# The last output tile of a fused attention and feed-forward kernel: three column pieces, each stored from two queues

## The chip, the cores and the metric

One core of one Trainium2 chip. The metric is the device time of one execution in microseconds (us); the profile's span of the same execution is 1.7 to 1.8 us shorter. Every set of timed runs of a version was taken on the same chip as runs of the kernel before, in turns.

## The reference

A linear attention with cosine weights, whose output is the input of a feed-forward block:

```python
# q, k, v: (8, 8, 576, 64)
q_p, k_p = phi(q), phi(k)                      # relu, times cos and sin of the position: 128 features
kv  = einsum('bhsf,bhsd->bhfd', k_p, v)
x   = einsum('bhsf,bhfd->bhsd', q_p, kv) / (einsum('bhsf,bhf->bhs', q_p, k_p.sum(2)) + 1e-6)
x   = x.transpose(0, 2, 1, 3).reshape(4608, 512)
h   = x @ w_in                                 # 512 -> 2048
out = (h / (1 + exp(-beta * h))) @ w_out       # 2048 -> 512, fp32, (4608, 512)
```

## The kernel before

The 4608 tokens pass in nine chunks of 512. For each chunk TensorE makes 16 groups of `h` (four matmuls of 512 columns each), ScalarE turns each into a bf16 activation tile `g_t`, and TensorE then makes four output tiles of 128 tokens (16 matmuls of 512 columns each). An output tile holds two groups of 64 tokens that lie in different rows of the result, so it is stored in two halves of 64 rows. TensorE leaves its results in a memory called PSUM (`ps` in the code); VectorE or ScalarE copies them from there to a tile `o_sb` in SBUF, the core's working memory, from which the stores take them. The very last tile of the last chunk is made in two column pieces of 256, so that the first piece can be copied out and stored while the second is computed:

```python
    def store(c, tt, o_sb, m0=0, m1=512):
        for hf in range(2):
            bb, n = divmod((c * TCH + tt * P) // HP + hf, NQ)
            eng = nc.sync if c >= 7 else nc.gpsimd
            eng.dma_start(out=out_v[bb, n][:, m0:m1], in_=o_sb[hf * HP : (hf + 1) * HP, m0:m1])
    # ... cut ...
    def o_last(c, tt):
        o_sb = osb_pool.tile([P, DM], FP32, name="o_sb", tag="o_sb")
        for hf in range(2):
            m0, m1 = 256 * hf, 256 * hf + 256
            o_ps = ps[:, 4 + hf, 0:256]
            for jt in range(JT):                                   # 16
                nc.tensor.matmul(o_ps, lhsT=gs[c, jt][:, tt * P : (tt + 1) * P],
                                 rhs=wout[jt // 4][:, jt % 4, m0:m1],
                                 start=(jt == 0), stop=(jt == JT - 1))
            (nc.scalar.copy if hf == 0 else nc.vector.tensor_copy)(o_sb[:, m0:m1], o_ps)
            store(c, tt, o_sb, m0, m1)
```

Of the kernel before, what the change touches and what calls it, by code (L numbers as in the profile page):

```python
# [22 lines left out]
def kernel(  # L23
# [14 lines left out]
    nc = tc.nc  # L38
# [26 lines left out]
    ps = psum.tile([P, 8, 512], FP32, name="ps")  # L65
# [313 lines left out]

    out_v = out.rearrange("(b p n) m -> b n p m", b=B, n=NQ)  # L380

    def store(c, tt, o_sb, m0=0, m1=512):
        for hf in range(2):
            bb, n = divmod((c * TCH + tt * P) // HP + hf, NQ)
            eng = nc.sync if c >= 7 else nc.gpsimd
            eng.dma_start(out=out_v[bb, n][:, m0:m1], in_=o_sb[hf * HP : (hf + 1) * HP, m0:m1])  # L386

    def o_part(c, tt, part):
        o_ps = ps[:, (2, 3, 0, 1)[tt] if c == 0 else 2 + tt % 2]
        for jt in range(4 * part, 4 * part + 4):  # L390
            nc.tensor.matmul(o_ps, lhsT=gs[c, jt][:, tt * P : (tt + 1) * P],  # L391
                             rhs=wout[jt // 4][:, jt % 4, :],
                             start=(jt == 0), stop=(jt == JT - 1))
        if part < 3:
            return
        o_sb = osb_pool.tile([P, DM], FP32, name="o_sb", tag="o_sb")
        nc.scalar.copy(o_sb, o_ps)  # L397
        store(c, tt, o_sb)

    def o_last(c, tt):  # L400

        o_sb = osb_pool.tile([P, DM], FP32, name="o_sb", tag="o_sb")
        for hf in range(2):
            m0, m1 = 256 * hf, 256 * hf + 256
            o_ps = ps[:, 4 + hf, 0:256]
            for jt in range(JT):
                nc.tensor.matmul(o_ps, lhsT=gs[c, jt][:, tt * P : (tt + 1) * P],  # L407
                                 rhs=wout[jt // 4][:, jt % 4, m0:m1],
                                 start=(jt == 0), stop=(jt == JT - 1))
            (nc.scalar.copy if hf == 0 else nc.vector.tensor_copy)(o_sb[:, m0:m1], o_ps)  # L410
            store(c, tt, o_sb, m0, m1)


    def warm_pe(count, w=512, bank=1):
# [170 lines left out]
    for c in range(1, NTC):  # L585
        units = att_units(c + 1) if c + 1 < B else []
        for slot in range(32):
            if c == 1 and slot < 4:
                h_mm(c, slot, (2, 3))
                h_act(c, slot)  # L590
            elif slot < 16:
                h_group(c, slot)
            elif c == NTC - 1 and slot >= 28:
                if slot == 28:
                    o_last(c, 3)
            else:
                o_part(c, (slot - 16) // 4, slot % 4)
            while units and units[0][0] <= slot:
                units.pop(0)[1]()
# [30 lines left out]
```

## Time and profile before

| | before |
|---|---|
| time, median of 3 runs | 296.96 us (296.57 to 296.97) |
| span of the profiled run | 294.99 us |
| TensorE busy | 97% of the span |
| last tile, first weight load to last matmul's end | 3.87 us |
| from there to the end of the span (the tail) | 4.21 us |

The prediction below shows the lines that carry this. In them, a chain line reads: start, length, what. A timeline line reads: start, length, engine, source line, operation, and in brackets how long the engine had been idle and who released it. "SPq" is SyncE's queue, "ACTq" ScalarE's; a DMA line's length is that of the issue, not of the transfer, whose end is given as "DMA to landing". "DVEq" is likewise VectorE's queue, here an instruction that only waits. A row of one source line reads: line, engine, operation, count, then shortest, median and longest duration in ns and the first and last start. A row of a stretch reads: from, to and length, the busy time of each engine with its number of instructions, the granted clock, and in the last two columns the DMA engines' share and GB/s. Where this document gives times to the nanosecond, they are read from the start, end and landing records of the same traces.

### The profile page before, as it was taken

How to read it: one execution, taken by the hardware profiler on the slowest of the kernel's cores; microseconds unless marked ns; L12 is line 12 of the kernel's file. 1: busy time of each engine (PE TensorE's matmuls, PEld its weight loads, DVE VectorE, ACT ScalarE, POOL GpSimd, SP SyncE). 2: the span in 40 equal slices, each digit the busy share in tenths (PEclk: the TensorE clock that was granted, in tenths of full speed). 3: DMA queues.
4: the chain of work that ended last, by engine and by line, in shares of the span. 5: the costliest groups of instructions: out<-in, count | busy, mean ns of one | idle time of the engine just before them, and what ended most of it. 6: DMA issues, size and time to landing. Idle time of an engine off the chain costs nothing.

```text
span 295.0 us, 7173 instructions
## 1 busy us (share of the span) xinstructions
PE 286.8 (97%) x3058; PEld 142.8 (48%) x3058; DVE 116.3 (39%) x296; ACT 140.1 (47%) x223; POOL 73.8 (25%) x88
## 2 busy tenths in 40 slices
PE   8799999999999999999999999999999999999994
PEld 7454455455445544454445544554455444444443
DVE  5989978662920293019500960077005000000000
ACT  5758826563247214731474137512760277137510
POOL 1350003252382026402550256015701210000000
PEclk9999999999999999999999999999999999999999
DMA  7999999597999089916992599139102810130033
GB/s 259 366 393 379 387 389 393 197 288 268 163 259 361 4 125 219 383 62 120 217 379 76 113 231 397 45 67 196 44 2 46 146 37 0 41 84 19 0 73 71
DMA packets 50256, 53.82 MB, mean 182 GB/s; under 512 B 30880, under 2 KB 31152, under 8 KB 50224
## 3 DMA queue, kind: packets, MB, share of 16 engines
q1 hardware_dynamic: 47504, 46.01, 51.6%
q0 software_dynamic: 2688, 7.34, 10.7%
q8 instruction: 24, 0.39, 0.6%
q14 instruction: 8, 0.07, 0.1%
q10 hardware_dynamic: 32, 0.01, 0.0%
HBM read 36.71 MB, written 9.44 MB: 156 GB/s over the span
## 4 chain that ended last, share of the span: by engine, by line
PE 85%; DVE 5%; DMA 5%; ACT 2%; issue 1%; DVEq 0%
PE ps L366 38%; PE ps L391 38%; DMA w_stage<-in_moe_w_out_dram 5%; DVE win L108 4%; PE ps L281 4%; PE ps L260 3%; PE ps L407 1%; PE ps L416 1%; ACT vb L213 1%; DVE qs L218 1%; DVE xs L303 0%; ACT g_t L373 0%; ACT rk L188 0%; PE ps L425 0%; PE ps L230 0%
## 5 line engine op out<-in xcount | busy, mean ns | idle before, releaser
L366 PE MATMUL ps<-xt,win 128*128 128x512 bf16 x576 | 128.1, 379 | 0.8 <-ACT g_t L373 0.5
L391 PE MATMUL ps<-wout,g_t 128*128 128x512 bf16 x560 | 124.5, 379 | 0.2 <-ACT wout L115 0.2
L373 ACT ACTIVATE g_t<-ps,beta 128x512 bf16<-128x512 f32 x144 | 98.4, 687 | 36.6 <-PE ps L366 36.6
L366 PEld LDWEIGHTS <-win 128*128 128x128 bf16 x576 | 55.3, 98 | 67.6 <-DVE win L108 1.4
L391 PEld LDWEIGHTS <-g_t 128*128 128x128 bf16 x560 | 53.9, 98 | 64.0 <-issue 0.4
L386 POOL DMA_DIRECT2D out_dram<-o_sb x56 | 36.5, 656 | 142.2 <-ACT o_sb L397 142.2
L397 ACT COPY o_sb<-ps 128x512 f32<-128x512 f32 x35 | 20.5, 586 | 98.2 <-PE ps L391 98.2
L218 POOL TENSOR_TENSOR qs<-qt,tanr 128x1152 bf16<-128x1152 bf16 x12 | 29.3, 2456 | 10.2 <-DMA qt<-qb 10.2
L272 DVE CAST kv<-ps 128x520 bf16<-128x520 f32 x6 | 4.2, 700 | 67.8 <-PE ps L260 67.8
L410 DVE COPY o_sb<-ps 128x256 f32<-128x256 f32 x1 | 0.4, 425 | 63.0 <-PE ps L407 63.0
L303 DVE TENSOR_TENSOR xs<-ps,rden 128x768 bf16<-128x768 f32 (+5 forms) x26 | 23.1, 890 | 0.8
L292 DVE TENSOR_TENSOR den<-ps,eps 128x12 f32<-128x12 f32 (+4 forms) x26 | 4.2, 161 | 33.5 <-PE ps L281 33.5
L215 DVE TENSOR_SCALAR vb<-raw_v,cos 128x256 bf16<-128x256 f32 x63 | 17.1, 347 | 0.0
L215 DVE TENSOR_SCALAR vb<-raw_v,sin 128x256 bf16<-128x256 f32 x54 | 14.7, 349 | 0.0
L281 PEld LDWEIGHTS <-qt 64*64 64x64 bf16 x576 | 10.6, 106 | 5.0 <-issue 4.3
L281 PE MATMUL ps<-kv,qt 64*64 64x65 bf16 x576 | 11.8, 195 | 0.4 <-ACT kv L270 0.2
L190 DVE TENSOR_SCALAR qb<-raw_q 128x1152 bf16<-128x1152 f32 x16 | 11.4, 752 | 1.3 <-DMA raw_q<-in_q_dram 1.3
L108 DVE CAST win<-w_stage 64x512 bf16<-64x512 f32 (+1 forms) x28 | 11.6, 414 | 0.6
L260 PE MATMUL ps<-vb,rk 64*64 64x130 bf16 x576 | 10.1, 218 | 1.6 <-ACT rk L188 1.6
L281 PE MATMUL ps<-kv,qs 64*64 64x65 bf16 x576 | 11.6, 193 | 0.0
L260 PEld LDWEIGHTS <-rk 64*64 64x64 bf16 x576 | 8.5, 106 | 5.7 <-issue 3.0
L281 PEld LDWEIGHTS <-qs 64*64 64x64 bf16 x576 | 10.4, 105 | 0.0
(56 smaller groups left out, 99.9 us busy)
## 6 DMA issues: line engine op xcount, KB each, us to landing
raw_v<-in_v_dram SPq DMA_DIRECT2D x7, 1152.0 KB, 10.2
raw_k<-in_k_dram SPq DMA_DIRECT2D x7, 1152.0 KB, 12.9
raw_q<-in_q_dram SPq DMA_DIRECT2D x7, 1152.0 KB, 7.4
out_dram<-o_sb POOLq DMA_DIRECT2D x56, 128.0 KB, 4.1
w_stage<-in_moe_w_out_dram SPq DMA_DIRECT2D x4, 1024.0 KB, 9.0
w_stage<-in_moe_w_in_dram SPq DMA_DIRECT2D x3, 1024.0 KB, 12.8
out_dram<-o_sb SPq DMA_DIRECT2D x14, 128.0 KB, 2.3
raw_q<-in_q_dram SPq DMA_DIRECT2D x2, 576.0 KB, 4.4
```

The costliest lines, as they stand in the source:

```text
L108: nc.vector.tensor_copy(o, a)
L190: nc.vector.tensor_scalar(dst, src, scalar1=0.0, scalar2=None, op0=ALU.max)
L215: nc.vector.tensor_scalar(o, a, scalar1=t[:, n : n + 1], scalar2=None, op0=ALU.mult)
L218: eng.tensor_tensor(dst.rearrange("q n (g p) -> q n g p", g=2), src.rearrange("q n (g p) -> q n g p", g=2), tanr[:, n0:n1].unsqueeze(2).to ...
L260: nc.tensor.matmul(t[jj * HP : (jj + 1) * HP, g], lhsT=rk[hs, n, 2 * jp + jj, :], rhs=vb[hs, n, 2 * jp + jj].rearrange("q s e -> q (s e)") ...
L281: nc.tensor.matmul(ps[cols, bank + jj, slot * E : (slot + 1) * E], lhsT=(qt, qs)[cs][rows, jp, n, cols], rhs=kv[rows, g, jp, cs, :], start ...
L303: nc.vector.tensor_tensor(o.rearrange("q j n s d -> q j (n s) d"), nv[:, :, a:z, :, 0:D].rearrange("q j n s d -> q j (n s) d"), rden[:, :, ...
L366: nc.tensor.matmul(ps[:, h_bank(c, jt)], lhsT=win[jt // 4][:, mi, (jt % 4) * P : (jt % 4 + 1) * P], rhs=xt[:, :, jp, g * HP : (g + 1) * HP ...
L373: nc.scalar.activation(g_t, ps[:, h_bank(c, jt)], AF.Silu, scale=beta[:, jt : jt + 1])
L386: eng.dma_start(out=out_v[bb, n][:, m0:m1], in_=o_sb[hf * HP : (hf + 1) * HP, m0:m1])
L391: nc.tensor.matmul(o_ps, lhsT=gs[c, jt][:, tt * P : (tt + 1) * P], rhs=wout[jt // 4][:, jt % 4, :], start=(jt == 0), stop=(jt == JT - 1))
L397: nc.scalar.copy(o_sb, o_ps)
```

## The change

Intent: with smaller last pieces, less is left to copy and to store when the last matmul is done; with one half on SyncE's queue and one on ScalarE's, the second half needs not wait for the first one's issue.

```diff
-    def store(c, tt, o_sb, m0=0, m1=512):
+    def store(c, tt, o_sb, m0=0, m1=512, two=False):
         for hf in range(2):
             bb, n = divmod((c * TCH + tt * P) // HP + hf, NQ)
-            eng = nc.sync if c >= 7 else nc.gpsimd
+            eng = (nc.sync, nc.scalar)[hf] if two else nc.sync if c >= 7 else nc.gpsimd
             eng.dma_start(out=out_v[bb, n][:, m0:m1], in_=o_sb[hf * HP : (hf + 1) * HP, m0:m1])
@@ o_last @@
-        for hf in range(2):
-            m0, m1 = 256 * hf, 256 * hf + 256
-            o_ps = ps[:, 4 + hf, 0:256]
+        for i, (m0, m1) in enumerate(((0, 256), (256, 384), (384, 512))):
+            o_ps = ps[:, 4 + i, 0 : m1 - m0]
             for jt in range(JT):
                 ...
-            (nc.scalar.copy if hf == 0 else nc.vector.tensor_copy)(o_sb[:, m0:m1], o_ps)
-            store(c, tt, o_sb, m0, m1)
+            (nc.scalar.copy if i == 1 else nc.vector.tensor_copy)(o_sb[:, m0:m1], o_ps)
+            store(c, tt, o_sb, m0, m1, two=True)
```

## The prediction

> **What bounds the kernel now.** I read the page's busy shares first, then the chain that ended last, then its last pieces in order of time, then the tail's rows one by one.
>
> The busy shares and the chain say what the body is bound by:
>
> ```profile
> span 295.0 us, 7173 instructions
> PE 286.8 (97%) x3058; PEld 142.8 (48%) x3058; DVE 116.3 (39%) x296; ACT 140.1 (47%) x223; POOL 73.8 (25%) x88
> ...
> PE 85%; DVE 5%; DMA 5%; ACT 2%; issue 1%; DVEq 0%
> ```
>
> TensorE is busy for 97% of the span and carries 85% of the chain. The change touches none of that body: only the last 128-row output tile (L407 to L411) and its stores. So all of the effect lies in the last 8 us. The chain in order of time gives their compute part:
>
> ```profile
> 276.93 10.36 PE ps L391 x48
> 287.29 3.51 PE ps L407 x32
> 290.80 0.03 DVEq L410
> 290.83 0.04 issue
> 290.88 0.42 DVE o_sb L410
> ```
>
> The last tile is 32 matmuls of 256 columns, 3.51 us or 109.7 ns each; then VectorE copies the second half out of PSUM, ending at 291.30. Here the chain of compute stops and the stores take over. The last two issues on SyncE's queue (a timeline of that queue for 291.3 to 291.6, then one of all engines for 291.5 to 292 and for 291.85 on), and the stores' own rows by stretch:
>
> ```profile
> 291.33 0.47 SPq L386 DMA_DIRECT2D out_dram<-o_sb  x1
> ...
> 291.85 0.59 SPq L386 DMA_DIRECT2D out_dram<-o_sb  x1
> ```
>
> ```profile
> L386 SPq DMA_DIRECT2D out_dram<-o_sb x1: 588/588/588, 291.8 to 291.8; - x1
> DMA to landing us min/median/max: 2.0/2.0/2.0
> ```
>
> The two 64-row halves are issued one after the other, 0.52 us apart; the second lands 2.0 us after its start, at 293.85. Five stretches of the tail show the rest:
>
> ```profile
> 292.44:293.00 0.56, 0.00 (x0) 0.00 (x0) 0.00 (x0) 0.00 (x0) 0.00 (x0) 1.00 0.49 117
> 293.00:293.40 0.40, 0.00 (x0) 0.00 (x0) 0.00 (x0) 0.00 (x0) 0.00 (x0) 1.00 0.62 148
> 293.40:293.85 0.45, 0.00 (x0) 0.00 (x0) 0.00 (x0) 0.00 (x0) 0.00 (x0) 1.00 0.06 14
> 293.85:295.00 1.15, 0.00 (x0) 0.00 (x0) 0.00 (x0) 0.00 (x0) 0.00 (x0) 1.00 0.00 0
> ```
>
> The last two columns are the DMA engines' share and GB/s: the bytes move between 292.44 and 293.4, so the issue itself and the confirmation, not the bandwidth, fill the 2.0 us. From 293.85 to 295.0 only closing waits, drains and semaphores run. The tail therefore adds up: 290.80 (last matmul) + 0.08 (hand-over) + 0.42 (copy) + 0.03 (hand-over) + 0.52 (first issue) + 2.0 (second store) + 1.15 (closing) = 295.0.
>
> **What the Trainium skill says.**
> - "DMA: Bandwidth & Descriptors", section "Issuing engines are not separate DMA queues": stores issued from several engines run on the same 16 DMA engines, and only the sequencer's issue time is saved. Here that time is the 0.52 us between the two issues; the trace of before never stores from two of these queues in the tail, so it can't confirm it.
> - "Perfetto Trace Analysis", section "DMA Instruction — HWDGE (DVE, Sync)": the block that generates descriptors is shared by the issuing sequencers and locked for exclusive use, and the profiled window includes the wait for the lock. If so, two stores issued at once partly queue. The trace hints at something like it: in each pair the second issue takes 587 to 589 ns against 466 of the first.
> - "TensorE: Matmul & The Clock Gate", section "Back-to-back issue gap": columns/2.4 + 2.5 ns apart when isolated (109 ns at 256 columns, which agrees with 109.7; 56 ns at 128), but some 81 ns per matmul in a real stream of weight load and matmul at 128 columns. The trace's own 128-column bursts decide below.
> - "VectorE: DVE Perf Modes", section on the TRN2 errata: a PSUM to SBUF copy costs a fixed term plus the columns. The trace agrees in kind: 425 ns at 256 columns on VectorE is far from twice a 128-column one.
>
> **The change part by part.**
> TensorE: piece one stays 16 matmuls of 256 columns. The other 16 become 32 of 128 columns: the same columns, but 16 more matmuls with 16 more weight loads. Their pace I take from the transposes, which also pair a 128-column weight load with a 128-column matmul:
>
> ```profile
> 44.31 0.67 PE L230 MATMUL ps<-ident,qb 128*128 128x128 bf16 x9
> ```
>
> ```profile
> L340 PEld LDWEIGHTS <-xs x32: 95/98/99, 16.3 to 52.7; 128*128 128x128 bf16 x32
> L340 PE MATMUL ps<-ident,xs x32: 218/219/230, 16.3 to 52.8; 128*128 128x128 bf16 x32
> ```
>
> Nine in 0.67 us, less one duration of 0.219, are eight gaps of 56 ns. Before: 31 gaps of 109.7 + 273 ns for the last = 3.67 us. After: 16 x 109.7 + 31 x 56.5 + 219 = 1755 + 1752 + 219 = 3.73 us. Cost: +0.06. At 81 ns a gap it would be +0.82. All on the path.
>
> Evacuation: only the last piece's copy is on the path. VectorE's PSUM copies took 169 ns at 16 columns and 425 ns at 256, so 1.07 ns a column, and 288 ns at 128: -0.14. ScalarE's two sizes (372 ns at 256, 586 at 512) give about 265 ns for the middle piece, and that is hidden: it ends some 0.6 us before the last piece's copy can end. VectorE takes piece one in place of ScalarE, 50 ns longer, hidden as well.
>
> Issues: the count rises from four to six. Those of pieces one and two lie beside matmuls. Piece two is in SBUF about 0.27 + 0.08 us after its last matmul, 0.9 us before the last matmul of all plus 0.35, so its pair of issues (0.47 to 0.59 us each, on two queues) is over about when the last pair wants to start; no queue should be occupied then, by a margin of some 0.3 us. For the last piece, both halves start together: -0.52 if fully parallel. I expect the shared block to give some back and put +0.2 on the second, between 0 and the 0.47 of a complete queueing.
>
> Size: each last store falls from 64 to 32 KB. The 128 KB stores landed in 2.2 to 2.4 us, the 64 KB ones in 1.9 to 2.1, so 0.3 for a halving of 64 KB; an estimate of -0.15 for the next 32 KB. Rows shrink from 1024 to 512 bytes, which may eat part of that.
>
> Closing: SyncE has more completions to wait for; each wait is 28 ns in the trace, so about +0.08 for three.
>
> Sum: +0.06 - 0.14 - 0.52 + 0.2 - 0.15 + 0.08 = -0.47 us on the span. The profiled run was 296.77 against a span of 295.0, so the same 1.8 us stay outside. 296.96 - 0.47 = 296.5.
>
> **The rivals.**
> 1. The smaller matmuls run at a real stream's pace, not at the transposes' 56 ns. For: the skill's figure of 81 ns, and that nine transposes are a short burst, with weights perhaps loaded ahead. Against: the warm-up's 58 matmuls of 48 columns, with their weight loads, ran in 2.50 us, 40 ns a pair, so neither weight loads nor dispatch limit at 56. Then the sum becomes +0.3: 297.25.
> 2. The lock makes the two queues serial: the second store starts its descriptors only when the first is through. Then 0.47 of the 0.52 comes back, the sum is -0.2: 296.75, about what one queue alone would give.
> 3. Fully parallel, with no contention: -0.67, 296.3.
> 4. ScalarE's sequencer is held by its own stores: piece two's copy waits behind piece one's issue. Piece one's issue ends about 1.1 us after its last matmul and piece two's matmuls end 0.9 us after it, so a delay of 0.2 us at most, with the last pair's start only just touched. Worth 0 to +0.2.
>
> **Range and chances.** The levers together reach from -0.7 (no lock cost) to +0.4 us (slow small matmuls and a lock). Repeated runs of before differ by 0.4 us, as large as the effect. I take 296.5 us with 295.9 to 297.2. Two per cent would be 5.9 us, more than the whole tail after the last matmul (4.2 us), so within 2% is all but sure: 0.99.
>
> **What would show each step.** The last tile's matmuls should take 3.7 us, the 128-column gaps 56 ns; gaps near 80 prove rival 1. The last VectorE copy should read about 290 ns. The last two issues, on SyncE and ScalarE, should start within 0.05 us of each other; if one is near 0.9 us long, or lands 0.4 us later than the other, rival 2 holds. The span should end near 294.5, with the closing part 1.15 to 1.25 us. I am wrong if the closing grows by much more than the 0.08 given to it, or if stores with 512-byte rows land later than the 2.0 us of before.

## The result, and the profile after

| | before | changed |
|---|---|---|
| time, median of 6 runs | 296.97 us (296.57 to 297.14) | 295.69 us (295.62 to 296.08) |
| mean of the same runs | 296.91 | 295.80 |
| span of the profiled run | 294.99 | 294.27 |

The ratio is 0.9963 (95% interval 0.995 to 0.9976). It is the mean time of the changed kernel's fast runs over that of the kernel before's fast runs of the same rounds, so not quite the ratio of the medians. The change is a gain of less than 2%, as foretold, but the time lies 0.2 us below the foretold range of 295.9 to 297.2 and 0.8 us below the foretold 296.5.

The chain of the changed kernel in order of time, its end:

```profile
287.27 3.55 PE ps L406 x48
290.81 0.02 issue
290.84 0.29 DVE o_sb L409
```

The last tile is now 48 matmuls, in 3.55 us of the chain where 32 took 3.51, and the last copy takes 0.29 in place of 0.42 us. The timeline of all engines at 291.1 to 291.2, and the rows of the stores that start there:

```profile
291.16 0.47 SPq L386 DMA_DIRECT2D out_dram<-o_sb  x1
291.16 0.74 ACTq L386 DMA_DIRECT2D out_dram<-o_sb  x1
```

```profile
L386 SPq DMA_DIRECT2D out_dram<-o_sb x1: 467/467/467, 291.2 to 291.2; - x1
L386 ACTq DMA_DIRECT2D out_dram<-o_sb x1: 738/738/738, 291.2 to 291.2; - x1
...
DMA to landing us min/median/max: 1.8/1.9/2.1
```

The two issues of the last piece, 0.52 us apart before, start together. One lands after 1.8 us, the other after 2.1; the latter is ScalarE's (1.769 and 2.073 us). The stretches of the tail, with the DMA share and GB/s in the last two columns as before:

```profile
291.16:292.30 1.14, 0.00 (x0) 0.00 (x0) 0.00 (x0) 0.00 (x0) 0.00 (x0) 1.00 0.37 87
292.30:292.90 0.60, 0.00 (x0) 0.00 (x0) 0.00 (x0) 0.00 (x0) 0.00 (x0) 1.00 0.45 106
292.90:293.23 0.33, 0.00 (x0) 0.00 (x0) 0.00 (x0) 0.00 (x0) 0.00 (x0) 1.00 0.00 0
293.23:294.27 1.04, 0.00 (x0) 0.00 (x0) 0.00 (x0) 0.00 (x0) 0.00 (x0) 1.00 0.00 0
```

The closing part, after the last landing, fell from 1.10 to 1.04 us. Step by step, from the last tile's first weight load to the end of the span:

| step | before | changed | difference | foretold |
|---|---|---|---|---|
| first weight load to last matmul's end | 3.871 | 3.910 | +0.04 | +0.06 |
| to the start of the last copy | 0.091 | 0.038 | -0.05 | none |
| last copy (VectorE) | 0.425 | 0.292 | -0.13 | -0.14 |
| to the first issue of the last pair | 0.029 | 0.027 | 0.00 | none |
| first to second issue | 0.518 | 0.005 | -0.51 | -0.52 |
| second store, issue to landing | 2.042 | 2.073 | +0.03 | +0.2 - 0.15 |
| last landing to the end of the span | 1.101 | 1.039 | -0.06 | +0.08 |
| sum | 8.077 | 7.384 | -0.69 | -0.47 |

Between the last matmul's end and the last copy the chain of before has two steps (`DVEq L410`, 0.03 us, and `issue`, 0.04, in the prediction's lines), the changed kernel's only the `issue` of 0.02 shown above.

So the two traces hold 0.69 us of gain in the last tile. The medians differ by 1.28 us and the means by 1.11. The first question to the experiments was where the rest came from; the second, what each part of the change is worth.

### The profile page after: what moved, and what is told of

It reads as the page before. It is cut to its first block, busy times and chain, and to the rows that moved or that the text cites. A ratio compares the mean times of both kernels' runs of the same rounds, so it can differ in the third digit from the quotient of the medians.

```text
span 294.3 us, 7183 instructions
## 1 busy us (share of the span) xinstructions
PE 284.1 (97%) x3046; PEld 143.2 (49%) x3074; DVE 116.6 (40%) x297; ACT 140.1 (48%) x223; POOL 73.8 (25%) x88
## 4 chain that ended last, share of the span: by engine, by line
PE 84%; DVE 5%; DMA 5%; ACT 2%; issue 2%
PE ps L366 38%; PE ps L391 37%; DMA w_stage<-in_moe_w_out_dram 5%; DVE win L108 4%; PE ps L281 4%; PE ps L260 3%; PE ps L406 1%; PE ps L415 1%; ACT vb L213 1%; DVE qs L218 1%; DVE xs L303 0%; ACT g_t L373 0%; ACT rk L188 0%; PE ps L424 0%; PE ps L230 0%
## 5 line engine op out<-in xcount | busy, mean ns | idle before, releaser
L391 PE MATMUL ps<-wout,g_t 128*128 128x512 bf16 x535 | 120.4, 379 | 2.5 <-issue 1.4
L409 DVE COPY o_sb<-ps 128x256 f32<-128x256 f32 (+1 forms) x2 | 0.7, 358 | 62.6 <-PE ps L406 62.6
```

## The experiments

"Tile to end" is the sum of the table above: first weight load of the last tile to the end of the span. "Timed" is the difference of the mean times to the runs of before of the same session; the ratios have their 95% interval in brackets.

### a_again, a_third, a_fourth, b_again: the same kernels once more

No edit: the changed kernel in three more sessions, and the kernel before timed against itself.

> The changed kernel once more, unaltered. Theory 1 (all of the gain is in the tail; what the timed runs showed beyond it is the spread from run to run): the gain in the timed runs is near the 0.72 us that the two traces show, the last output tile again starts near 287.1 us, and the time from the last matmul's end to the end of the span is 3.4 to 3.6 us. Theory 2 (the change also shortens something ahead of the tail in most runs): the timed gain stays at 1.1 us or more, and this trace's last tile starts 0.3 us or more earlier than 287.1.

> The changed kernel a third time, for the size of the gain. Theory 1 (only the tail changes, by 0.72 us, and the start of the last tile moves by up to half a microsecond from run to run in every kernel alike): the tail of this trace is again 3.47 us within 0.05, and the gain of all timed runs pooled is 0.6 to 0.9 us. Theory 2 (something ahead of the tail gained too) expects pooled 1.0 us or more.

> The changed kernel on the same chip and beside the same runs of before as the version above. Tile to end again 7.38 us; timed 0.7 us under before within the session's spread, and 0.25 to 0.35 us over the version above if that version's steps hold.

> The kernel before, unaltered, timed against itself. So far its tail was read from one trace (4.21 us from the last matmul's end, 8.08 us from the last tile's first weight load). If the gain beyond the tail's 0.70 us is only spread between runs, this trace shows the same two figures within 0.03 us, and the two sets of timed runs of one and the same kernel differ by up to 0.4 us in their means. If the tail of before is itself variable and longer as a rule, the figures are 0.15 us or more larger.

| run | tile starts at | tile to end | tail after last matmul | timed | ratio |
|---|---|---|---|---|---|
| before (first trace) | 286.91 | 8.077 | 4.206 | | |
| b_again (before) | 286.57 | 8.074 | 4.204 | +0.01 | 1.0003 [0.9987, 1.0019] |
| changed (first trace) | 286.89 | 7.384 | 3.474 | -1.11 | 0.9963 [0.995, 0.9976] |
| a_again (changed) | 287.32 | 7.383 | 3.472 | -0.53 | 0.9978 [0.9965, 0.9992] |
| a_third (changed) | 286.88 | 7.366 | 3.455 | -0.95 | 0.9967 [0.9951, 0.9982] |
| a_fourth (changed) | 287.06 | 7.361 | 3.450 | -0.91 | 0.997 [0.9957, 0.9983] |

The last tile repeats within 0.03 us, in both kernels; with that, and with means 0.01 us apart, b_again came out as foretold. What differs is when the tile starts. (Three marks of this start are in use: the table's first weight load; the first matmul, some 0.2 us later, to which the 287.1 us of the expectations belongs; and the tile's first line in the chain, another 0.2 us later.) The line of the last tile's matmuls in the chains of b_again, of a_again and of two_last (an experiment below whose body is the same too):

```profile
286.95 3.51 PE ps L407 x32
```

```profile
287.70 3.55 PE ps L406 x48
```

```profile
286.80 3.51 PE ps L407 x32
```

In the first pair of traces it started at 287.29 and 287.27. The same program, ahead of a tile that no version changes, comes to it up to 0.9 us earlier or later. The traces part early in the body, where it waits for loads: at 5 to 8 us by up to 0.3 us, and again at 44 to 46 us, when the output weights are due; the chain's next `h` matmuls then start at 51.60 us in the first trace of before, at 51.17 in b_again, 51.24 in two_last and 51.81 in a_again. The kernel before waited there, by its own row of TensorE's waits; the row is absent in b_again and in two_last, which start the last tile 0.34 and 0.49 us earlier:

```profile
PE ps L391 <- ACT wout L115: 0.2, 1, 0.2
```

(The 0.2 us are TensorE's own idle time there, only a part of the shift. The row alone does not tell early from late: it is also absent in two_only and act_last, which start the tile 0.18 and 0.14 us later than the first trace of before. What sets the start is not settled.)

So the expectation of theory 1 held for the tail in all four traces of the changed kernel, and theory 2's, a first matmul 0.3 us or more earlier than 287.1, in none (287.09 to 287.54). That does not refute theory 2 for the other executions: the traced ones took 296.08, 296.52, 296.05 and 296.19 us, each above the mean of its session, the first two the slowest of theirs. The ten executions of 295.53 to 295.71 us, a group of their own among the 22, left no trace. If the tile took its 7.37 us in them, it started near 286.4 us (an estimate: 295.6 less 1.8 outside the span and 7.37), as early as in two_last (286.43), which has the body of before. The timed gains range from 0.53 to 1.11 us for one and the same pair of kernels. Pooled, 22 runs of the changed kernel have a mean of 295.95 us and 54 of before 296.86: a gain of 0.91 us, give or take 0.17 if all runs are taken as independent (0.87 against the runs of before of the same four sessions alone). That is at the upper edge of what a_third named for theory 1 (0.6 to 0.9) and 0.2 us more than the 0.70 us that the last tile gives. With the interval as wide as it is, this remainder is barely clear of zero. If the tile repeats as in the traces, it lies in an earlier start of the tile in executions that were not traced; whether the change causes that or chance does stays open.

### two_only and two_last: the second queue without the smaller pieces

Both keep the two pieces of 256. In two_only both pieces are stored from two queues, in two_last only the second:

```diff
-            eng = nc.sync if c >= 7 else nc.gpsimd
+            eng = (nc.sync, nc.scalar)[hf] if two else nc.sync if c >= 7 else nc.gpsimd
...
-            store(c, tt, o_sb, m0, m1)
+            store(c, tt, o_sb, m0, m1, two=True)          # two_only
+            store(c, tt, o_sb, m0, m1, two=hf == 1)       # two_last
```

> The last tile stays in two pieces of 256, only the second half of each store moves to the ScalarE queue. If the second queue is what pays: the issues start together (-0.52 us) and the gain is 0.25 us (the ScalarE issue again 0.74 us long, because simultaneous issues exclude each other) up to 0.5 us (the ScalarE issue near 0.5 us, because the 0.74 came from the pair issued just before, which here is over 1.2 us earlier). If the pieces are what pays, the gain is under 0.15 us.

> Two pieces of 256; the first stored by SyncE alone, only the second by both queues. If the long ScalarE issue (0.74 us) was a backlog of the pair before, it is near 0.5 us here and the gain is 0.4 to 0.5 us; if simultaneous issues exclude each other, it is again near 0.74 and the gain about 0.25 us.

The last pair's rows in two_only and in two_last:

```profile
L386 SPq DMA_DIRECT2D out_dram<-o_sb x1: 467/467/467, 291.5 to 291.5; - x1
L386 ACTq DMA_DIRECT2D out_dram<-o_sb x1: 497/497/497, 291.5 to 291.5; - x1
...
DMA to landing us min/median/max: 1.9/2.1/2.2
```

```profile
L386 SPq DMA_DIRECT2D out_dram<-o_sb x1: 467/467/467, 290.8 to 290.8; - x1
L386 ACTq DMA_DIRECT2D out_dram<-o_sb x1: 548/548/548, 290.8 to 290.8; - x1
...
DMA to landing us min/median/max: 1.9/2.1/2.2
```

Tile to end: 7.762 and 7.764 us, a gain of 0.31 each. Timed: -0.29 us, 0.9989 [0.9977, 1.0002], which is not clear of noise, and -0.46 us, 0.9984 [0.9971, 0.9996]. The long ScalarE issue of 0.74 us is gone (0.50 and 0.55), so it goes with a pair that follows another pair after 0.64 us, as the backlog theory had it. But the gain of 0.4 to 0.5 us that I tied to that did not come. In each simultaneous pair ScalarE's store lands 0.26 to 0.30 us after SyncE's (2.202 against 1.939 us in two_only), whether its issue reads 0.50 or 0.74 us. The length of the issue says nothing about the landing here. Of the 0.51 us saved between the issues, 0.16 came back in the second landing (2.202 against 2.042 us) and 0.04 in the closing.

### act_last: is it the queue or the company?

> Two pieces of 256; of the last piece both stores come from the ScalarE queue, one after the other, so nothing is issued at the same time. It takes apart why the ScalarE store of each simultaneous pair landed 0.27 to 0.30 us after the SyncE one (2.07 against 1.77 us from issue to landing). If the ScalarE queue is slower by itself, its first store here takes some 2.2 us to land; if simultaneous issues hold each other up, it takes the 1.92 us that the first SyncE store of before took. In the first case the tail is 0.1 to 0.3 us longer than before's 4.21 us, in the second about the same.

```diff
-            eng = (nc.sync, nc.scalar)[hf] if two else ...
+            eng = nc.scalar if two else ...                # two only for the last piece
```

The row of ScalarE's first store of the last pair:

```profile
L386 ACTq DMA_DIRECT2D out_dram<-o_sb x1: 546/546/546, 291.5 to 291.5; - x1
...
DMA to landing us min/median/max: 2.0/2.0/2.0
```

Alone it lands after 2.005 us, between the two expectations: 0.08 us later than SyncE's first store of before (1.925), and 0.20 us earlier than the 2.20 us that it takes beside SyncE's. So of the lag of some 0.27 us, some 0.08 goes with ScalarE's queue and 0.20 with the company of the other store. (The SyncE store of the pair hardly pays: 1.939 us against 1.925. No run swapped the two queues, so whether ScalarE's pays because it is ScalarE's or because it is issued 4 ns later stays open.) The second one, issued 0.59 us after the first, lands after 2.056 us. Tile to end 8.142 (before 8.077), timed +0.08, 1.0001 [0.9985, 1.0018].

### three_only: the smaller pieces without the second queue

```diff
-            store(c, tt, o_sb, m0, m1, two=True)           # from the changed kernel
+            store(c, tt, o_sb, m0, m1)
```

> Three pieces of 256, 128 and 128 with all stores on the SyncE queue. Theory 1 with the issue times of the traces: six issues of 0.47 and 0.59 us in a row from 289.56 us on keep the queue busy until about 291.75, so the last pair starts 0.6 us after its data are ready and lands near 294.2: slower than before by 0.2 to 0.4 us. A rival, that the smaller last copy and the smaller last stores pay by themselves, expects a gain of 0.15 to 0.3 us.

The last two issues on SyncE's queue (timelines of that queue from 291.9 and from 292.5):

```profile
291.95 0.55 SPq L386 DMA_DIRECT2D out_dram<-o_sb  x1
```

```profile
292.54 0.59 SPq L386 DMA_DIRECT2D out_dram<-o_sb  x1
```

The data of the last piece were in place at 291.04. Its first store starts 0.91 us later, behind the four issues of the pieces before, and its second 1.51 us later. Tile to end 8.605 us, 0.53 longer than before; timed +0.49 us, 1.0016 [1.0003, 1.0028]. The rival, that small pieces pay by themselves, is refuted: on one queue they cost half a microsecond. The delay is even larger than I expected, as the issues lie 0.52 to 0.68 us apart. (This trace's mean granted clock was 0.993 where the others have 0.999 to 1.000; the last tile took its 3.91 us of the changed kernel all the same.) With the second queue the same pieces improve two_only's 7.762 to 7.384 us. The two parts of the change are thus not two gains that add: the second queue alone gains 0.31 us, the small pieces alone lose 0.53, and together they gain 0.69.

### one_store: one issue in place of two

For the last chunk ScalarE writes the activations so that the two groups of 64 tokens alternate. An output tile's 128 rows then go out in one store:

```diff
+        if c == NTC - 1:
+            o = g_t.rearrange("q (t p h) -> q t h p", t=TT, h=2)
+            a = a.rearrange("q (t h p) -> q t h p", t=TT, h=2)
+        nc.scalar.activation(o, a, AF.Silu, scale=beta[:, jt : jt + 1])
...
+        if c == NTC - 1:                                    # store()
+            eng.dma_start(out=out_v[bb, n : n + 2].rearrange("n p m -> p n m")[:, :, m0:m1], in_=o_sb[:, m0:m1])
```

> For the last 512 tokens the two 64-row halves are interleaved row by row (ScalarE writes the activations in that order), so that each piece of 128 rows goes out in one issue on the SyncE queue instead of two. Two pieces of 256 as before. If the gain of the second queue was only that the second issue no longer waits 0.52 us for the first, one issue does the same without a second queue: the tail is 0.3 to 0.5 us shorter than before's 4.21 us, as with two queues (3.89 us). If the number of 64-row descriptor sets is what takes the time, the one store of 128 rows lands about 2.3 us after its issue; if the number of issues does, about 2.0 us.

```profile
L389 SPq DMA_DIRECT2D out_dram<-o_sb x1: 539/539/539, 291.4 to 291.4; - x1
...
DMA to landing us min/median/max: 2.1/2.1/2.1
```

With two pieces of 256 and no second queue, tile to end is 7.393 us, as short as the changed kernel's; timed -0.61 us, 0.9977 [0.9959, 0.9996]. The tail is 3.523 us, 0.68 under before where I expected 0.3 to 0.5. The one store of 128 rows lands after 2.060 us, near the 2.0 for "the number of issues" and 0.14 us sooner than the later of two_only's pair, which moves the same bytes. The closing shrank to 0.918 us, which makes 0.18 of the gain that I had not expected; it is taken up under "Wrong" below.

### best and best2: the version to which the steps point

> The version to which the steps point: pieces of 384 and 128 columns (16 matmuls fewer than three pieces, an estimate of 0.06 us), each copied half by VectorE and half by ScalarE (the last copy 64 columns each, about 0.22 us in place of 0.29), each piece in one interleaved store, the first from the SyncE queue, the last from the ScalarE queue. Tail from the last matmul's end to the end of the span 3.3 to 3.5 us against 3.47 of the changed kernel and 4.21 of before; start of the last tile to the end of the span about 0.1 to 0.2 us under the changed kernel's 7.17 us. In the timed runs 0.7 to 1.0 us under before.

In best, each piece was copied half by VectorE and half by ScalarE, in the hope that they work side by side. The timeline shows that they don't:

```profile
291.35 0.23 DVE L418 COPY o_sb<-ps 128x64 f32<-128x64 f32 x1 [0.55 <-PE ps L414]
291.61 0.21 ACT L419 COPY o_sb<-ps 128x64 f32<-128x64 f32 x1 [0.46 <-DVE o_sb L418]
```

ScalarE is released by VectorE's copy, not by TensorE: as built, the second copy into the same tile waits for the first. Two halves one after the other are slower than one copy. Tile to end 7.397 us, no better than the changed kernel; timed -0.62 us, 0.9978 [0.996, 0.9995]. My expectation of 0.1 to 0.2 us less failed on that, and so did the 0.7 to 1.0 us foretold for the timed runs. (The 7.17 us in it are the changed kernel's from the first matmul on; from the first weight load they are 7.384.) best2 removes the split:

```diff
-            w = (m1 - m0) // 2
-            nc.vector.tensor_copy(o_sb[:, m0 : m0 + w], o_ps[:, 0:w])
-            nc.scalar.copy(o_sb[:, m0 + w : m1], o_ps[:, w : 2 * w])
-            store(c, tt, o_sb, m0, m1, nc.scalar if i else nc.sync)
+            (nc.vector.tensor_copy if i == 0 else nc.scalar.copy)(o_sb[:, m0:m1], o_ps)
+            store(c, tt, o_sb, m0, m1)                      # pieces (0, 384) and (384, 512)
```

> Pieces of 384 and 128 columns, each in one interleaved store on the SyncE queue; VectorE copies the first, ScalarE alone the last (the split copy of the version before ran one engine after the other). By the steps measured so far: TensorE 3.87 us from the last tile's first weight load, as with two pieces of 256; hand-over, a copy of 0.266 us and hand-over, so the last issue starts about 0.37 us after the last matmul's end; one store of 64 KB, 1.9 us to land; closing 0.92 us. Tail 3.1 to 3.3 us, tile to end 7.0 to 7.15 us, 0.95 us under before and 0.25 to 0.35 us under the changed kernel. If instead the closing or the landing grows back, the tail stays near 3.5 us. The timed gain should be 0.95 us give or take the 0.4 us by which a session's mean moves.

Its stretches, from the last matmul's end to the last issue, to the landing, to the end:

```profile
290.72:291.13 0.41, 0.00 (x0) 0.00 (x0) 0.00 (x0) 0.27 (x1) 0.00 (x0) 1.00 0.00 0
291.13:293.06 1.93, 0.00 (x0) 0.00 (x0) 0.00 (x0) 0.00 (x0) 0.00 (x0) 1.00 0.40 136
293.06:293.98 0.92, 0.00 (x0) 0.00 (x0) 0.00 (x0) 0.00 (x0) 0.00 (x0) 1.00 0.00 0
```

Tail 3.256 us and tile to end 7.127 us, both as expected: 0.95 under before, 0.23 to 0.26 under the changed kernel, the low edge of what I foretold. The last store landed after 1.923 us; the same store from ScalarE's queue in best took 2.021, so that queue is again the slower by some 0.1 us, with no other store issued at the same time. Timed -1.20 us, 0.9961 [0.9949, 0.9973]. In the same session the changed kernel's mean was 296.09 and this version's 295.81; with runs that scatter by 0.3 us, six of each, that difference of 0.28 us is not clear of noise by itself. It rests on the traces.

## Why the prediction was right or wrong

**Right: the place and most terms.** The gain lies in the last tile, and of the foretold terms three came within 0.02 us: the matmuls (56 ns apart at 128 columns, so the transposes were a fair measure of the pace and rival 1 with its 81 ns fell), the last copy (0.292 against 0.288 us), and the two issues' start together. The two guesses on the second store held as a sum: +0.05 foretold, +0.03 measured. They held singly too: the simultaneous store from ScalarE's queue landed 0.16 us later than the second store of before (2.202 in two_only against 2.042) where I put 0.2, and halving its bytes took 0.13 us off (2.073) where I put 0.15. Rival 2, complete queueing, fell: the lag between the two landings is 0.27 to 0.30 us, not 0.47, and some 0.08 us of it is there without company (act_last). Rival 3, no contention, fell with it. The aside in rival 2, that 0.2 us is about what one queue alone would give, was wrong: three_only lost 0.53. Rival 4, ScalarE held by its own stores, did not happen: its copy starts at 290.23, its first store's issue having ended at 290.11. The margin of some 0.3 us before the last pair was thinner, though: the issues of the pair before ended at 290.985 and 291.022, 0.17 and 0.14 us ahead of it.

**Wrong: "Closing ... about +0.08 for three."** It measured -0.06, the largest error of the sum (0.14 us). I took more stores to mean more waits after the last landing. SyncE's closing waits are a fixed list that it walks in order, some 60 ns from one to the next, and those before the last landing are worked off while the data are still under way. What counts is how many stand behind the wait for the store that lands last. The counts from the last landing on, its own wait among them, are 4 before and 3 in the changed kernel:

```profile
L625 SPq EVENT_SEMAPHORE  x4: 28/28/28, 293.9 to 294.1; - x4
```

```profile
L624 SPq EVENT_SEMAPHORE  x3: 28/28/28, 293.2 to 293.4; - x3
```

In two_only they are 5, in three_only 2:

```profile
L625 SPq EVENT_SEMAPHORE  x5: 28/28/28, 293.7 to 294.0; - x5
```

```profile
L624 SPq EVENT_SEMAPHORE  x2: 28/28/28, 294.5 to 294.5; - x2
```

The closing goes along: 1.140 us with 5, 1.101 with 4, 1.039 with 3, 0.965 with 2. The other traces fall in line: 1.140 with 5 in two_last, 1.100 and 1.081 with 4 in b_again and act_last, 1.019 to 1.039 with 3 in the changed kernel's three more, and 0.898 to 0.918 with 1 in one_store, best and best2. No run changed the order alone, but all thirteen traces fit it within about 0.02 us.

**Wrong by omission: the hand-over from TensorE.** I took 0.08 us for it on both sides. It was 0.091 us before and is 0.038 now, so that matmuls and hand-over together give -0.01 us where I had +0.06. The matmuls' ends are modelled, but TensorE's signal of the last matmul is recorded, 14 ns after the modelled end in both traces, and the difference lies behind it: 77 ns from the signal to the copy before, 24 now. Before, VectorE took the signal with a wait of its own (`DVEq L410`); in the changed kernel it had made its other waits for its copy of the first piece, and the last copy waits for TensorE alone. All thirteen traces agree: 0.08 to 0.11 us where the chain has such a wait in front of the last piece's first copy (eight), 0.04 where it has none (the changed kernel's four and three_only). So giving VectorE the first piece too, which I counted as hidden, paid some 0.05 us; no run changed that alone.

The closing's 0.14 us and the 0.07 us of matmuls and hand-over together make 0.21 of the 0.22 us by which the sum was too small.

**Wrong: a fixed start of the last tile, and so the range.** These two terms alone would not have put the time outside the range: 296.97 less the tile's 0.69 us is 296.3. What did is a step that the prediction took without saying so. From "The change touches none of that body" it took the time up to the last tile as the same number in both sets of runs and put the tile's gain straight onto the median ("296.96 - 0.47 = 296.5"). The traces show the tile starting up to 0.9 us earlier or later (thirteen traces), and three runs of before within 0.4 us had shown too little of it. "The levers together reach from -0.7 ... to +0.4 us. Repeated runs of before differ by 0.4 us, as large as the effect": the range should have been the levers and the scatter together. The low end of 295.9 is the levers' best case plus 0.36 us of slack, and the first session passed it. (The levers were not added up rightly either: slow small matmuls and a lock, by the prediction's own sums for rivals 1 and 2, make +0.56 and not +0.4; neither came true.) For the first session the account is: 0.69 us in the tile, and a remaining 0.42 us of the means' difference that no step of the tile explains. The later sessions, with 0.53, 0.95 and 0.91 us, show that much of it is scatter, so that the first miss was partly bad luck. Over all sessions the changed kernel's mean is 295.95 us, just inside the range; why the pooled gain is 0.2 us larger than the tile's stays open.

## What to carry to other kernels

At the end of a kernel count issues before bytes: here two half stores on one queue cost 0.52 us, two queues gave back 0.2 us of it in a later landing and closing, and a layout that lets one store take all rows saved the same without a second queue. Count also the waits that stand behind the last landing (some 60 ns each here). Smaller pieces pay only if the queue can issue them in time. And where the effect is a few tenths of a microsecond, compare the changed stretch in several traces, not the totals: the stretch repeated within 0.03 us while the totals of the same pair of kernels put its gain anywhere from 0.5 to 1.1 us.

## What the Trainium skill lacked or had wrong

- "DMA: Bandwidth & Descriptors", section "Issuing engines are not separate DMA queues", says that a second issuing engine saves only the issue time, usually small beside the transfer. It saved 0.51 us here, a quarter of the 2.04 us that the store took to land, and the page has no figure for what the company costs: the ScalarE store landed after 2.20 us beside a SyncE one and after 2.005 us alone.
- The same page, section "Rules for kernel authors", advises one 128-partition transfer in place of two halves, with no figure for what it is worth. That agrees: one store landed after 2.06 us where the later of two simultaneous halves took 2.20 us.
- "Perfetto Trace Analysis", section "DMA Instruction — HWDGE (DVE, Sync)", counts the wait for the shared block in the profiled window. The runs add that the window's length does not foretell the landing: issues of 0.498 and 0.738 us landed after 2.050 and 2.073 us.
- "TensorE: Matmul & The Clock Gate", section "Back-to-back issue gap", gives some 81 ns for matmuls of 128 columns in a stream with weight loads. 32 of them, each with its weight load, ran 56 ns apart here, which is its figure for the isolated gap.
- No page has the time that a program's own closing waits take: here 0.90 to 1.14 us from the last landing to the end of the span, some 60 ns for each completion that is waited for behind the last one to land.
